# Queries and normalised x of items two to four transposed by DMA instead of TensorE, in a fused attention and maxout kernel

## The chip, the cores and the metric

The kernel runs on one core of a Trainium2 chip. The metric is device time in microseconds, the median of several executions. Lower is better. One execution is also taken by the profiler; all durations and waits below come from that one.

## What is computed

The input is a batch of 4 items with 8 heads, 768 tokens and 64 columns per head, and a sorting matrix of 8 by 8 per item and head. The reference, cut to what matters:

```python
for _ in range(5):                       # sort_net, 8x8 per head
    P = exp(P - max); P = P / rowsum; P = P / colsum
k_sorted = einsum('bhij,bhjcd->bhicd', P, k_b)   # blocks of 96 tokens mixed
v_sorted = einsum('bhij,bhjcd->bhicd', P, v_b)
scores = scale * matmul(q_b, k_sb^T)     # within a block of 96
attn = softmax(scores)
x = matmul(attn, v_sb)                   # -> 3072 tokens x 512
h1 = x @ w1; h2 = x @ w2
out = maximum(h1, h2) @ w_out            # float32, 3072 x 512
```

The kernel computes the last part as relu(x (w1 - w2)) @ w_out + x (w2 @ w_out). Products are in bfloat16 with float32 accumulation.

## The kernel before

The four items follow each other as a software pipeline. While TensorE does the dense products of item b (`moe_h`, the first layer, and `moe_out`, the second), it does the attention of item b+1 in between. The order is written out by hand: the loop at the end of the kernel has a list of `units` for item b (eight `moe_h`, then `moe_out` in halves of six products) with a cost each, and a list of `steps` for item b+1; after each unit so many steps are issued as the share of the units' cost that has passed asks for. `tail` holds steps that are tied to a certain unit, among them what is left of the item before. [...]PSUM is one pool of four tiles of two banks each, shared by all products, so a product waits when all four still wait for their eviction. `pick` shares the evictions out to ScalarE and VectorE by a running estimate of their load.

The steps of one item, with the lines before the change:

- `load_q` (L127), `load_k`, `load_v`: loads from DRAM on GpSimd's queue, which change float32 to bfloat16 on the way. There is one buffer for `q_raw` and one for `q_pair`, so the load of an item's queries waits for the pairing of the item before.
- `pair_q` (L322): VectorE copies the heads so that two heads that share a row group lie side by side: `q_pair` is 128 token groups by 4 head pairs by 6 rows by 128 columns. A partition holds six tokens that follow each other (R = 6).
- `sort_k`, `sort_v`, `sort_v_pair` (L365 to L428): the mixing of blocks on TensorE. `turn_v` (L203) turns the layout of v for it on VectorE or ScalarE.
- `q_transposes` (L332): 12 transposes on TensorE for each half of the heads into one PSUM tile, then one eviction into `qT`. In `qT` a block's 96 tokens lie as six groups of 16 (r, c).
- `scores` (L432): eight products of 96 columns into PSUM, then the exponential on ScalarE into an `e` tile. Its columns keep the (r, c) order.
- `values` (L458): eight products with the sorted v and a column of ones; then VectorE takes the reciprocal of the sum (L477) and multiplies (L483) into an `x` tile. An `x` tile serves two head pairs; the pool has three.
- `x_transposes` (L491): eight transposes on TensorE of 96 by 128, then an eviction into `xT` that also puts the tokens back in order (c, r).

Item one differs: its queries are transposed straight from `q_raw` at L349, and the kernel's beginning is written out without units.

`moe_h` of item b reads the first half of `xT` from its first unit on and the second half from unit five on. `moe_out` ends with an eviction into an `o` tile (three buffers) and a store of 512 KB on SP's queue (L613). Before the change SP's queue has one load and these stores alone.

In the steps of items two to four the values come as six groups inside the stage; the last two groups of values and the last two x transposes of an item stand in `tail`, in units 0, 1 and 2 of its own dense stage:

```python
tail = {0: [VA[6], VA[7]], 1: [TR[2]], 2: [TR[3]]}
```

Of the kernel before, what the change touches and what calls it, by code (L numbers as in the profile page):

```python
# [9 lines left out]

FP32 = mybir.dt.float32
BF16 = mybir.dt.bfloat16


@with_exitstack
def kernel(
# [16 lines left out]
    nc = tc.nc  # L33
# [4 lines left out]
    B, H, S, D = q.shape  # L38
    NB = sort_net.shape[-1]
    BLK = S // NB  # L40
# [5 lines left out]
    R = S // 128  # L46
    PB = 128 // NB
    HP = H // 2
    HB = BLK // 2
    TCH = S // 2  # L50
# [14 lines left out]
    def ps_f32(name):  # L65
        return psum.tile([128, 1024], FP32, tag="ps", name=name)

    def ps_bf16(name):
        return psum.tile([128, 2048], BF16, tag="ps", name=name)

# [5 lines left out]
    def keep_streaming(ps, n, by=None, width=512):  # L76

        w0 = fill[:, 0:128] if by is None else late[by]
        while n > 0:
            w = min(n, width)  # L80
            nc.tensor.matmul(ps[:, 0:w], w0, fill[:, 0:w], start=True, stop=True)  # L81
            n -= w
# [28 lines left out]
    q_raw, qT = {}, {}  # L111
# [10 lines left out]
    for n in range(NE):  # L122
        t = big.tile([BLK, 8 * BLK + 32], BF16, tag=f"e{n}", name=f"e{n}")
# [52 lines left out]
    ident = const.tile([128, 128], BF16, tag="ident", name="ident")  # L176
# [26 lines left out]
    def turn_v(rows, eng, c0, c1, d0=0, d1=D):  # L203
        dst = v_dc[rows, 0 : D * BLK].rearrange("p (d c) -> p d c", c=BLK)[:, d0:d1, c0:c1]
        src = v_raw[rows].rearrange("p (c d) -> p d c", d=D)[:, d0:d1, c0:c1]
        if eng == "A":
            nc.scalar.copy(out=dst, in_=src)
        else:
            nc.vector.tensor_copy(out=dst, in_=src)  # L209


    rowsum = const.tile([G, NB], FP32, tag="rowsum", name="rowsum")
# [107 lines left out]
    q_pair = {}  # L320
# [8 lines left out]
        )  # L329
        load["D"] += 900  # L330

    def q_transposes(b, half, eng=None, n=0):  # L332

        if half == 0:
            qT[b] = qpool.tile([128, HP, R, 128], BF16, tag="qT", name="qT")
        ps = ps_f32("tq_ps") if n else ps_bf16("tq_ps")
        keep_streaming(ps, n)
        if n:
            ps = ps.bitcast(BF16)
        for m in range(2 * R):  # L340
            hp, r = half * 2 + m // R, m % R
            c = slice(m * 128, (m + 1) * 128)
            if b in q_pair:
                nc.tensor.matmul(  # L344
                    ps[:, c], q_pair[b][:, hp, r], ident, is_transpose=True, start=True, stop=True
                )
                continue
            for h2 in range(2):
                nc.tensor.matmul(  # L349
                    ps[h2 * 64 : h2 * 64 + 64, c],  # L350
                    q_raw[b][:, hp + 4 * h2, r * D : (r + 1) * D],
                    ident,
                    is_transpose=True,
                    start=True,
                    stop=True,
                )
        evac(
            qT[b][:, half * 2 : half * 2 + 2].rearrange("p h r c -> p (h r c)"),
            ps[:, 0 : 2 * R * 128],
            2 * R * 128,  # L360
            two_x=True,
            eng=eng,
        )
# [68 lines left out]
    def scores(b, u, n=0):  # L432
        ih, hp = divmod(u, HP)
        ps = ps_f32("s_ps")
        keep_streaming(ps, n)
        for ii in range(4):
            i = ih * 4 + ii
            for h2 in range(2):
                rows = slice(h2 * 64, h2 * 64 + 64)
                rhs = qT[b][rows, hp, :, i * PB : (i + 1) * PB]  # L440
                nc.tensor.matmul(  # L441
                    ps[:, h2 * 512 + ii * BLK : h2 * 512 + (ii + 1) * BLK],
                    kT[b][rows, (hp * 8 + i) * BLK : (hp * 8 + i) * BLK + 128],
                    rhs,
                    start=True,
                    stop=True,
                )
        e = e_bufs[(b * 8 + u) % NE]
        nc.scalar.activation(  # L449
            out=e[:, 0 : 8 * BLK].rearrange("p (t f) -> p t f", t=2),  # L450
            in_=ps[0:BLK].rearrange("p (t f) -> p t f", t=2)[:, :, 0 : 4 * BLK],
            func=AF.Exp,
            scale=scale,
        )
        load["A"] += 800
        e_tiles[b, u] = e

    def values(b, u, n=0):  # L458
        ih, hp = divmod(u, HP)
        e = e_tiles.pop((b, u))  # L460
        m0 = (b % 2) * 64
        ps = ps_f32("o_ps")
        keep_streaming(ps, n)
        for h2 in range(2):
            for ii in range(4):
                nc.tensor.matmul(  # L466
                    ps[:, h2 * 512 + ii * 65 : h2 * 512 + (ii + 1) * 65],
                    e[:, (h2 * 4 + ii) * BLK : (h2 * 4 + ii) * BLK + 128],
                    v_sb[:, m0 + (hp + 4 * h2) * 8 + ih * 4 + ii, 0:65],
                    start=True,  # L470
                    stop=True,
                )
        ov = ps[0:BLK].rearrange("p (t f) -> p t f", t=2)[:, :, 0 : 4 * 65].rearrange(
            "p t (i f) -> p t i f", f=65
        )
        rs = xpool.tile([BLK, 2, 4], FP32, tag="rs", name="rs")
        nc.vector.reciprocal(out=rs, in_=ov[:, :, :, 64])  # L477
        if hp % 2 == 0:
            x_tiles[b, ih, hp // 2] = xpool.tile(
                [BLK, 2, 4, 2, D], BF16, tag="x", name="x", bufs=3  # L480
            )
        x = x_tiles[b, ih, hp // 2][:, :, :, hp % 2, :]
        nc.vector.tensor_tensor(  # L483
            out=x,
            in0=ov[:, :, :, 0:D],
            in1=rs.to_broadcast([BLK, 2, 4, D]),
            op=ALU.mult,
        )
        load["D"] += 900

    def x_transposes(b, t, eng=None):  # L491

        ih, hh = divmod(t, 2)
        ps = ps_bf16("tx_ps")
        x = x_tiles.pop((b, ih, hh))
        for m in range(8):
            h2, ii = divmod(m, 4)
            nc.tensor.matmul(  # L498
                ps[:, h2 * 1024 + ii * BLK : h2 * 1024 + (ii + 1) * BLK],
                x[:, h2, ii].rearrange("p n d -> p (n d)"),  # L500
                ident[0:BLK, 0:BLK],
                is_transpose=True,
                start=True,
                stop=True,
            )

        dst = xT[:, b % 2, ih, hh].rearrange("p h (i c r) -> p h i c r", r=R, c=PB)
        src = ps.rearrange("p (h f) -> p h f", h=2)[:, :, 0:TCH].rearrange(
            "p h (i r c) -> p h i c r", r=R, c=PB
        )  # L510
        evac(dst, src, 2 * TCH, eng=eng)


    w2T = big.tile([128, NFB, DMODEL], BF16, tag="w2T", name="w2T")
# [212 lines left out]
    for b in range(B):  # L727
# [25 lines left out]
        if b < B - 1:  # L753
            qs = [lambda half=half: q_transposes(b + 1, half) for half in range(2)]
            pairs = [lambda two=two: pair_q(b + 1, two) for two in range(2)]
            ks = [lambda t=t, b=b: sort_k(b + 1, t) for t in range(3)]
            SC, VA, TR = att(b + 1)

            def group(*fs):
                return [lambda: [f() for f in fs]]  # L760

            if b == 0:
                lo = 10
                tail[9][2:2] = ks
                vs = [lambda t=t: sort_v(1, t) for t in range(4)]
                tns = [lambda c=c: turn(both, c) for c in range(0, BLK, 12)]
                VA[1:6] = [(lambda f=f, g=g: (f(), g())) for f, g in zip(VA[1:6], tns)]
                TR[0:2] = [(lambda f=f, g=g: (f(), g())) for f, g in zip(TR[0:2], tns[5:])]
                SC[7:] = [lambda f=SC[7], g=tns[7]: (f(), g())]
                steps = group(*vs[:3]) + qs[:1] + group(*SC[0:2], vs[3]) + qs[1:] + VA[:1]  # L770
                steps += group(*SC[2:5]) + VA[1:2]
            elif b == 1:
                vs = [lambda t=t: sort_v_pair(2, t) for t in range(8)]
                steps = group(*pairs) + group(*ks) + qs[:1] + group(*SC[0:2], vs[0]) + qs[1:]
                steps += group(*vs[1:4]) + group(*vs[4:7]) + group(*SC[2:4], vs[7]) + VA[:2]
            else:
                steps = group(*pairs) + group(*ks) + qs + group(*SC[0:2])
                steps += VA[:1] + group(*SC[2:5]) + VA[1:2]
            rest = SC[4:] if b == 1 else SC[5:]
            steps += VA[2:3] + TR[:1] + VA[3:4]  # L780
            steps += group(*rest[:-1]) + TR[1:2] + VA[4:5] + rest[-1:] + VA[5:6]
        done = 0
        for n, unit in enumerate(units):
            unit()
# [4 lines left out]
            while done < min(want, len(steps)):  # L789
                steps[done]()  # L790
                done += 1
        tail = {0: [VA[6], VA[7]], 1: [TR[2]], 2: [TR[3]]}
        if b == 0:
            tail[3] = [lambda: load_k(3)]
            tail[8] = [lambda: load_q(3)]
# [28 lines left out]
```

The softmax here doesn't subtract the row's maximum and nothing guards it: scores larger than these inputs give would overflow.

## Time and profile before

| what | value |
|---|---|
| median of 3 runs | 178.54 us (178.17 to 178.55) |
| profiled execution | 178.51 us |
| its span in the trace | 176.5 us |
| instructions | 4808 |
| DMA queue 0 (loads, GpSimd) | 10304 packets, 12.58 MB, 42.4% of 16 engines |
| DMA queue 1 (SP) | 3328 packets, 6.10 MB, 9.1% of 16 engines |

The profiled execution's time is 2.0 us longer than its span: that part lies around the instructions of the trace. A row of instruction groups gives the line, the engine, the operation, output and input tiles with their shapes and the count; then the busy time in us and the mean ns of one; then the idle time of that engine just ahead of the group and what ended it. PE is TensorE's products, PEld its weight loads, DVE is VectorE, ACT is ScalarE, POOL is GpSimd, SP is SyncE, which has a queue of DMAs alone here. A timeline row begins with its start and its length in us. In the row of DMA digits each digit is a slice of a fortieth of the span, in tenths of full.

### The profile page before, as it was taken

Reading aid. Unit: us, or ns where it says so; the run is one execution under the profiler, and the core shown is the slowest. Engines: PE = TensorE matmul, PEld = TensorE weight load, DVE = VectorE, ACT = ScalarE, POOL = GpSimd, SP = SyncE. Lnnn points to the kernel's source line nnn. Section 1 sums busy time; section 2 is a strip of 40 time slices with the busy share of each in tenths; the row PEclk is TensorE's granted clock in tenths of the full one; section 3 lists DMA queues with packets and bytes.
Section 4 is the critical chain, followed back from the end, with each engine's and each line's share of the span. In section 5 each row is a group of like instructions: output and inputs, shape, how many; then the busy total and the mean of one; then the engine's idle time right before and its main releaser. Section 6 shows DMA issues by size and latency. Waiting matters only on the chain.

```text
span 176.5 us, 4808 instructions
## 1 busy us (share of the span) xinstructions
PE 169.4 (96%) x2159; PEld 105.1 (60%) x2159; DVE 95.3 (54%) x201; ACT 91.1 (52%) x110; POOL 24.1 (14%) x39
## 2 busy tenths in 40 slices
PE   7999999999999999999989999999999999999993
PEld 7848675655765554577655454677555546654453
DVE  4979758688555697354586435346325426240210
ACT  3689957854663655277783341474833232630021
POOL 7855353110730000020000000000000000000000
PEclk9999999999999999999999999999999999999999
DMA  4999999999799962039200203300001132000333
GB/s 55 200 205 208 198 207 215 201 203 210 114 214 212 206 176 108 16 119 148 38 0 4 97 26 119 119 6 4 0 0 62 61 119 111 12 0 0 119 116 125
DMA packets 13940, 19.19 MB, mean 109 GB/s; under 512 B 800, under 2 KB 8864, under 8 KB 13920
## 3 DMA queue, kind: packets, MB, share of 16 engines
q0 software_dynamic: 10304, 12.58, 42.4%
q1 hardware_dynamic: 3328, 6.10, 9.1%
q8 instruction: 17, 0.28, 0.6%
q10 hardware_dynamic: 288, 0.20, 0.3%
q14 instruction: 3, 0.02, 0.0%
HBM read 25.17 MB, written 6.29 MB: 178 GB/s over the span
## 4 chain that ended last, share of the span: by engine, by line
PE 84%; DVE 9%; ACT 4%; issue 1%; DMA 1%; ACTq 0%
PE out_ps L593 36%; PE h_ps L566 23%; PE o_ps L466 4%; PE k_ps L374 4%; PE wc_ps L544 4%; PE tx_ps L498 3%; PE s_ps L441 3%; PE tq_ps L344 2%; PE v_ps L395 2%; DVE g L582 1%; ACT w2T L103 1%; PE tw_ps L521 1%; DMA p_sb<-in_sort_net_dram 1%; PE tq_ps L349 1%; DVE x L483 1%
## 5 line engine op out<-in xcount | busy, mean ns | idle before, releaser
L593 PE MATMUL out_ps<-wo_sb,g 128*128 128x512 bf16 (+2 forms) x208 | 48.1, 363 | 0.3 <-DVE g L582 0.2
L566 PE MATMUL h_ps<-xT,w_sb 128*128 128x384 bf16 x256 | 45.8, 326 | 0.4 <-DVE g L582 0.2
L566 PEld LDWEIGHTS <-w_sb 128*128 128x128 bf16 x256 | 23.8, 98 | 15.1 <-issue 0.2
L449 ACT ACTIVATE e<-s_ps 96x768 bf16<-96x768 f32 x32 | 24.2, 803 | 12.2 <-PE s_ps L441 12.0
L580 ACT ACTIVATE g<-h_ps 128x768 bf16<-128x768 f32 x22 | 17.7, 811 | 21.8 <-PE h_ps L566 21.7
L593 PEld LDWEIGHTS <-g 128*128 128x128 bf16 x208 | 17.9, 97 | 15.9 <-issue 0.2
L593 PE MATMUL out_ps<-wc,xT 128*128 128x512 bf16 (+2 forms) x104 | 25.0, 362 | 0.0
L103 ACT COPY o<-out_ps 128x1024 f32<-128x1024 f32 x8 | 8.1, 1013 | 29.3 <-PE out_ps L593 25.6
L483 DVE TENSOR_TENSOR x<-o_ps,rs 96x512 bf16<-96x512 f32 x32 | 22.0, 687 | 1.1
L477 DVE RECIPROCAL rs<-o_ps 96x8 f32<-96x8 f32 x32 | 6.4, 201 | 25.5 <-PE o_ps L466 25.4
L582 DVE TENSOR_SCALAR g<-h_ps 128x768 bf16<-128x768 f32 x10 | 9.6, 957 | 15.7 <-PE h_ps L566 15.6
L593 PEld LDWEIGHTS <-xT 128*128 128x128 bf16 x104 | 9.9, 97 | 10.9
L209 DVE COPY v_dc<-v_raw 64x768 bf16<-64x768 bf16 (+2 forms) x18 | 15.6, 897 | 0.5 <-DMA v_raw<-in_v_dram 0.4
L466 PEld LDWEIGHTS <-e 96*128 96x128 bf16 x256 | 11.0, 98 | 5.6 <-ACT e L449 0.5
L466 PE MATMUL o_ps<-v_sb,e 96*128 96x65 bf16 x256 | 12.4, 193 | 0.3 <-DVE x L483 0.2
L103 ACT COPY xT<-tx_ps 128x768 bf16<-128x768 bf16 x13 | 10.4, 798 | 4.5 <-PE tx_ps L498 4.5
L105 DVE CAST v_sb<-v_ps 96x1024 bf16<-96x1024 f32 x7 | 8.5, 1215 | 5.3 <-PE v_ps L395 3.3
L103 ACT CAST v_sb<-v_ps 96x1024 bf16<-96x1024 f32 x9 | 8.7, 1014 | 2.3 <-PE v_ps L395 1.4
L103 ACT CAST kT<-k_ps 128x1024 bf16<-128x1024 f32 x10 | 9.6, 1026 | 0.5 <-PE k_ps L374 0.5
L441 PEld LDWEIGHTS <-kT 64*128 64x128 bf16 x256 | 6.1, 94 | 5.4 <-issue 4.6
L129 POOL DMA_DIRECT2D q_raw<-in_q_dram x4 | 3.6, 902 | 39.8 <-DVE q_pair L326 37.4
L81 PEld LDWEIGHTS <-fill 128*128 128x128 bf16 x109 | 7.7, 128 | 2.2 <-DVE fill L72 1.2
(77 smaller groups left out, 166.1 us busy)
## 6 DMA issues: line engine op xcount, KB each, us to landing
out_dram<-o SPq DMA_DIRECT2D x11, 512.0 KB, 2.8
k_raw<-in_k_dram POOLq DMA_DIRECT2D x12, 256.0 KB, 14.0
q_raw<-in_q_dram POOLq DMA_DIRECT2D x4, 768.0 KB, 9.7
v_raw<-in_v_dram POOLq DMA_DIRECT2D x6, 384.0 KB, 12.5
w_sb<-in_moe_w_dram POOLq DMA_DIRECT2D x3, 512.0 KB, 15.7
wo_sb<-in_moe_w_out_dram POOLq DMA_DIRECT2D x2, 512.0 KB, 19.4
v_raw<-in_v_dram POOLq DMA_DIRECT2D x3, 256.0 KB, 5.1
w_sb<-in_moe_w_dram POOLq DMA_DIRECT2D x2, 256.0 KB, 14.3
```

Source lines behind the costliest of these rows:

```text
L81: nc.tensor.matmul(ps[:, 0:w], w0, fill[:, 0:w], start=True, stop=True)
L103: nc.scalar.copy(out=out_ap, in_=in_ap)
L105: nc.vector.tensor_copy(out=out_ap, in_=in_ap)
L209: nc.vector.tensor_copy(out=dst, in_=src)
L441: nc.tensor.matmul(ps[:, h2 * 512 + ii * BLK : h2 * 512 + (ii + 1) * BLK], kT[b][rows, (hp * 8 + i) * BLK : (hp * 8 + i) * BLK + 128], rhs ...
L449: nc.scalar.activation(out=e[:, 0 : 8 * BLK].rearrange("p (t f) -> p t f", t=2), in_=ps[0:BLK].rearrange("p (t f) -> p t f", t=2)[:, :, 0 ...
L466: nc.tensor.matmul(ps[:, h2 * 512 + ii * 65 : h2 * 512 + (ii + 1) * 65], e[:, (h2 * 4 + ii) * BLK : (h2 * 4 + ii) * BLK + 128], v_sb[:, m0 ...
L483: nc.vector.tensor_tensor(out=x, in0=ov[:, :, :, 0:D], in1=rs.to_broadcast([BLK, 2, 4, D]), op=ALU.mult,)
L566: nc.tensor.matmul(h_ps[t][:, m * 512 : m * 512 + TCH], w1_sb[:, hp, fb * 128 : (fb + 1) * 128], xT[:, b % 2, ch, hp % 2, hp // 2, :], sta ...
L580: nc.scalar.activation(out=g, in_=src, func=AF.Relu)
L582: nc.vector.tensor_scalar(out=g, in0=src, scalar1=0.0, scalar2=None, op0=ALU.max)
L593: nc.tensor.matmul(dst, g_tiles[b, ch, m // 2][:, m % 2, off : off + 128] if m < NFB else xT[:, b % 2, ch, hp % 2, hp // 2, off : off + 12 ...
```

## The change

For items two to four the query transposes and the x transposes become DMA transposes on SP's queue, from SBUF to SBUF: one DMA per half of the heads for the queries (128 by 1536), one per `x` tile (96 by 1024). The products, their PSUM tiles and their evictions go. [...]the exponential now reads PSUM at a stride and writes `e` in token order, for all four items; x and `xT` then are in token order too, so item one's eviction of `xT` is a straight copy. Each of the eight score products gets its own 128 columns of PSUM instead of 96. The `x` pool has four tiles instead of three. The last two values groups and x transposes of items two to four move from `tail` into the item's own steps. `turn_v` gets a repeat count of 1, and `q_transposes` loses a parameter that no call uses.

```diff
     def turn_v(rows, eng, c0, c1, d0=0, d1=D):
...
+        for _ in range(TWICE):
+            if eng == "A":
+                nc.scalar.copy(out=dst, in_=src)
+            else:
+                nc.vector.tensor_copy(out=dst, in_=src)
...
-    def q_transposes(b, half, eng=None, n=0):
+    def q_transposes(b, half, eng=None):
 
         if half == 0:
             qT[b] = qpool.tile([128, HP, R, 128], BF16, tag="qT", name="qT")
-        ps = ps_f32("tq_ps") if n else ps_bf16("tq_ps")
-        keep_streaming(ps, n)
-        if n:
-            ps = ps.bitcast(BF16)
+        if b in q_pair:
+            nc.sync.dma_start_transpose(
+                out=qT[b][:, half * 2 : half * 2 + 2].rearrange("p h r c -> p (h r) c"),
+                in_=q_pair[b][:, half * 2 : half * 2 + 2].rearrange("p h r e -> p (h r e)"),
+            )
+            return
+        ps = ps_bf16("tq_ps")
         for m in range(2 * R):
...
-            if b in q_pair:
-                nc.tensor.matmul(
-                    ps[:, c], q_pair[b][:, hp, r], ident, is_transpose=True, start=True, stop=True
-                )
-                continue
...
-                    ps[:, h2 * 512 + ii * BLK : h2 * 512 + (ii + 1) * BLK],
+                    ps[:, h2 * 512 + ii * 128 : h2 * 512 + ii * 128 + BLK],
...
         nc.scalar.activation(
-            out=e[:, 0 : 8 * BLK].rearrange("p (t f) -> p t f", t=2),
-            in_=ps[0:BLK].rearrange("p (t f) -> p t f", t=2)[:, :, 0 : 4 * BLK],
+            out=e[:, 0 : 8 * BLK].rearrange("p (t c r) -> p t c r", t=8, r=R),
+            in_=ps[0:BLK].rearrange("p (t f) -> p t f", t=8)[:, :, 0:BLK].rearrange(
+                "p t (r c) -> p t c r", r=R
+            ),
...
-                [BLK, 2, 4, 2, D], BF16, tag="x", name="x", bufs=3
+                [BLK, 2, 4, 2, D], BF16, tag="x", name="x", bufs=4
...
         ih, hh = divmod(t, 2)
+        x = x_tiles.pop((b, ih, hh))
+        if b > 0:
+            nc.sync.dma_start_transpose(
+                out=xT[:, b % 2, ih, hh].rearrange("p h (i c) -> p (h i) c", c=BLK),
+                in_=x.rearrange("p h i n d -> p (h i n d)"),
+            )
+            return
         ps = ps_bf16("tx_ps")
...
-        dst = xT[:, b % 2, ih, hh].rearrange("p h (i c r) -> p h i c r", r=R, c=PB)
-        src = ps.rearrange("p (h f) -> p h f", h=2)[:, :, 0:TCH].rearrange(
-            "p h (i r c) -> p h i c r", r=R, c=PB
-        )
-        evac(dst, src, 2 * TCH, eng=eng)
+        src = ps.rearrange("p (h f) -> p h f", h=2)[:, :, 0:TCH]
+        evac(xT[:, b % 2, ih, hh], src, 2 * TCH, eng=eng)
...
+            steps[-1:] = group(steps[-1], TR[2]) + VA[6:7] + group(VA[7], TR[3])
...
-        tail = {0: [VA[6], VA[7]], 1: [TR[2]], 2: [TR[3]]}
+        tail = {}
```

More of the change, by code (lines that the diff above doesn't have):

```diff
@@ L12 @@
 BF16 = mybir.dt.bfloat16
+TWICE = 1
 @with_exitstack
@@ L205, in turn_v @@
         src = v_raw[rows].rearrange("p (c d) -> p d c", d=D)[:, d0:d1, c0:c1]
[L206 to L209, printed above, removed]
+        for _ in range(TWICE):
[3 more added lines that the diff above has]
+                nc.vector.tensor_copy(out=dst, in_=src)
     rowsum = const.tile([G, NB], FP32, tag="rowsum", name="rowsum")
@@ L493, in x_transposes @@
         ih, hh = divmod(t, 2)
+        x = x_tiles.pop((b, ih, hh))
[5 more added lines that the diff above has]
+            return
         ps = ps_bf16("tx_ps")
-        x = x_tiles.pop((b, ih, hh))
         for m in range(8):
```

## The prediction, made before the changed kernel was run

> **What bounds the kernel now.** I read the page's busy shares, then idle TensorE time by stage, then the order of work where items meet, then the groups the change touches, then DMA.
>
> ```profile
> PE 169.4 (96%) x2159; PEld 105.1 (60%) x2159; DVE 95.3 (54%) x201; ACT 91.1 (52%) x110; POOL 24.1 (14%) x39
> ...
> DMA  4999999999799962039200203300001132000333
> ```
>
> TensorE is busy 96% of the span, VectorE and ScalarE about half. The DMA digits (slices of 4.4 us) stay at 9 until about 57 us and rise to 9 again at 75 to 80. Busy share alone doesn't prove a bound; the stages do. Columns: length, PE, PEld, DVE, ACT, POOL busy, granted clock, DMA share, GB/s:
>
> ```profile
> 44.00:62.00 18.00, 17.65 (x306) 11.22 (x303) 10.63 (x16) 10.16 (x12) 4.62 (x8) 1.00 1.04 187
> ...
> 73.00:90.00 17.00, 16.61 (x297) 11.84 (x296) 8.71 (x12) 12.99 (x15) 0.90 (x1) 1.00 0.43 79
> ...
> 108.00:128.00 20.00, 19.65 (x287) 13.17 (x286) 8.99 (x15) 11.50 (x15) 0.00 (x0) 1.00 0.12 44
> ```
>
> In each, the stages in which items two to four are transposed, at most 0.4 us of TensorE is idle at full clock. So a product removed there is time removed, as long as nothing new makes TensorE wait. The timeline of the second such stage (start, length, engine, line, tiles):
>
> ```profile
> 76.36 0.51 PE L498 MATMUL tx_ps<-ident,x 96*128 96x96 bf16 x8
> 76.69 1.01 DVE L326 COPY q_pair<-q_raw 128x1536 bf16<-128x1536 bf16 x2
> 76.70 1.47 PE L566 MATMUL h_ps<-xT,w_sb 128*128 128x384 bf16 x8
> ...
> 78.00 0.90 POOL L129 DMA_DIRECT2D q_raw<-in_q_dram  x1 [28.05 <-DVE q_pair L326]
> ...
> 81.38 0.83 PE L344 MATMUL tq_ps<-ident,q_pair 128*128 128x128 bf16 x12
> ...
> 82.05 1.46 PE L566 MATMUL h_ps<-xT,w_sb 128*128 128x384 bf16 x8
> ...
> 83.53 0.52 PE L441 MATMUL s_ps<-qT,kT 64*128 64x96 bf16 x16
> ```
>
> Start to start, an x transpose group costs TensorE 76.70 - 76.36 = 0.34 us, half a query transpose 82.05 - 81.38 = 0.67. The scores that need the queries come only 2.1 us after. The next load of q goes out as soon as the pairing is done.
>
> ```profile
> L449 ACT ACTIVATE e<-s_ps 96x768 bf16<-96x768 f32 x32 | 24.2, 803 | 12.2 <-PE s_ps L441 12.0
> L580 ACT ACTIVATE g<-h_ps 128x768 bf16<-128x768 f32 x22 | 17.7, 811 | 21.8 <-PE h_ps L566 21.7
> L103 ACT COPY xT<-tx_ps 128x768 bf16<-128x768 bf16 x13 | 10.4, 798 | 4.5 <-PE tx_ps L498 4.5
> ...
> out_dram<-o SPq DMA_DIRECT2D x11, 512.0 KB, 2.8
> ...
> out_dram<-o SPq DMA_DIRECT2D x1, 64.0 KB, 1.7
> ```
>
> L103 reads PSUM in a permuted order, L580 straight: 798 and 811 ns for 768 columns, so the permuted read is free. A store lands 1.7 us (64 KB) to 2.8 us (512 KB) after its issue; I take 1.6 as fixed.
>
> [...]No DMA transpose is in this trace.
> - [...]In this stream TensorE needs 670/12 = 56 ns[...]
> - [...]
> - [...]the store at 61.0, beside loads, lands after 4.7 us instead of 2.8. It has 16 packets of 2 KB per DMA engine, and a load packet takes 116 ns (queue 0: 42.4% of 16 x 176.5 us over 10304): 16 x 0.116 = 1.9.
> - [...]
>
> **The change, part by part.**
>
> *Removed from TensorE.* Twelve x groups (items two to four, four each), at 0.34 to 0.44 us in the timeline: 4.2 us. Six query halves: 0.67, 0.70, 0.67, 0.67, and 1.34 for the last two: 4.05. Together 8.3 us, all on the path. Their evictions (twelve of about 0.8, six of 0.95 to 1.44) leave ScalarE and VectorE: nothing on the path, as both are half idle.
>
> *Exponentials.* 32 of 803 ns, now read at a stride: 0 by the L103 row. At 0.1 us more each, 3.2 us would lie on ScalarE, idle half the time; without that cover it would be 3.2. The contiguous xT copy of item one and the repeat count of 1: nothing.
>
> *Added on SP's queue: six query transposes (393 KB[...]) and twelve of x (197 KB[...]).* Landing time H of a query half: 1.6 fixed plus data. [...]I take 4.2, [...]a second half follows H - 1.6 later. [...]An x transpose: 2.9.
>
> *When the halves are due*, in the built instruction order:
> - Item two: pairing ends at 45.05 and SP has nothing ahead. Scores at 51.54 - 0.67 - 0.16 idle = 50.7. Landing 45.05 + 4.2 + 0.7 = 49.95. Second half 52.85; wanted at 54.2. No wait.
> - Item three: the pairing now stands right after the previous values, but SP's transposes stand behind the stage's last output store. Counted from the last output product: eviction 1.0 + issue 0.4, store issued; transposes at 1.8. The 2.7 us between that and the end of the store's data (4.7 - 1.6 - 0.4, beside the q load) hold back about 2.0 beyond their own start-up: landing 1.8 + 4.2 + 0.7 + 2.0 = 8.7. Scores at three h units 3.9 + sorting of keys 1.63 + two units 2.6 = 8.1. TensorE waits 0.6.
> - Item four: no load beside it, store data short: landing 1.8 + 0.1 + 4.2 = 6.1, due at 9.4; second half 8.7, due at 12.3. No wait.
>
> *x.* The last x group lands 0.9 (VectorE) + 2.9 after its values; due six units (7.8 us) or more later. SP waits for x with output stores behind it, but three output buffers cover about 1 us, and no engine waits for a store. Cost 0, and that of the fourth x buffer also 0; if cover were gone, 2.9 per group.
>
> *Moved.* The last two values groups of an item go from the next stage into its own: same products, no net cost. Steps come denser: six sort_v_pair fills now follow each other. They take 6 x 0.29 = 1.8 us, the evictions (1.01 on ScalarE, 1.22 on VectorE) three rounds of about 1.1; four PSUM tiles hold a part. I estimate 1.1 of waits against two of 0.24 now: +0.6 (bounds 0 and 1.5).
>
> *New lateness in item two.* VectorE's first second-pair turn (L209, 59.55) needs a v load issued at 47.3 that lands 11.5 us later, at 58.8. The two query halves take 0.79 MB from DMA engines that are full (about 0.21 MB/us written, twice that read): loads land 0.9 to 1.8 later. TensorE comes 1.4 earlier. VectorE waits, and behind that turn stand the x normalisations that free PSUM. I take 0.9 (bounds 0 and 2).
>
> *Sum.* Profiled execution 178.5 us (span 176.5 and 2.0 around it), 0.03 from the median 178.54, so no correction: 178.5 - 8.3 + 0.6 + 0.6 + 0.9 = 172.3. Low end: nothing given back, 170.2.
>
> **Rivals.**
> - *Half the gain is eaten (175.2).* H = 5.5: item two waits 0.55 for its first half and 1.0 for the second, item three 1.3 more: 172.3 + 2.85. [...]Against: nothing in the trace.
> - *The crossbar is slow (183.7, slower).* The place is the scores (L441) behind qT. At H = 7.4 [...]item two waits 2.45 and 2.9, item three 3.2 more than counted, item four 2.8 for its second half: 172.3 + 11.4. The waits reach 6.2 and cancel the gain at H of about 6.4; from there it is slower. [...]
> - *Blocks one after another (about 225).*[...]
> - *Nothing changes (178.5).* The removed products were covered anyway; the 0.4 us of idle time speaks against it.
>
> **Chances.** Forecast 172.3: 0.47, own range 170.2 to 174. Half eaten: 0.13. Slow crossbar: 0.29. Serial blocks: 0.08. Unchanged: 0.03. Within 0.2% is about what a measurement of this kernel can't tell from no change. Faster 0.60, same 0.03, slower 0.37. The range runs from 170.2 to 190, the slow case with H up to about 8; beyond lie the serial blocks and a little more.
>
> **What would show it.** Right: no tq_ps group, tx_ps in item one alone, TensorE idle under 1 us before any L441 group, query halves landing in 4 to 5 us. Wrong: waits for DMA ahead of the scores, a PE clock under 1, ScalarE's exponentials well over 803 ns, or, if landing is fast and little is gained, PSUM waits for VectorE around 60 us.

## The result, and the profile after it

The changed kernel takes 194.67 us (median of 4 runs, 194.04 to 196.8) against 178.49 for the kernel before in the same comparison. The ratio is 1.093, 95% interval 1.085 to 1.102: slower, and beyond the end of the predicted range (190). The profiled execution took 194.95 us, its span 192.9 us, 16.4 longer than before. Where one of a kernel's runs was over 1.5% slower than its fastest, its median below leaves that run out. Lines of the changed kernel are five or so further on than before: the products of `h_ps` are L571, those of `out_ps` L598; the scores are still L441.

From the page of the changed kernel: busy shares, granted clock, DMA share by slice (of 4.8 us here), SP's DMA queue, and two groups.

```profile
PE 163.8 (85%) x1972; PEld 97.7 (51%) x1991; DVE 87.2 (45%) x192; ACT 83.4 (43%) x101; POOL 23.0 (12%) x39
...
PEclk9999999999978556999996999999999999999998
DMA  4999999999999940536995002555900336300223
...
q1 hardware_dynamic: 22336, 10.82, 23.8%
...
L449 ACT ACTIVATE e<-s_ps 96x768 bf16<-96x768 f32 x32 | 24.2, 803 | 35.4 <-PE s_ps L441 35.2
...
L441 PE MATMUL s_ps<-qT,kT 64*128 64x96 bf16 x256 | 9.1, 211 | 18.2 <-DMA qT<-q_pair 17.9
```

TensorE is busy 85% instead of 96%. TensorE's idle time grew from 7.1 to 29.1 us, and one group has most of the growth: 18.2 us ahead of the scores, 17.9 of it ended by the DMA that transposes the queries. The exponentials take 803 ns as before, so reading PSUM at this stride cost nothing here. The clock, 9 throughout before, drops to 7, 8, 5, 5, 6 between 53 and 77 us, and to 6 at 101 us. And SP's queue has 22336 packets where it had 3328.

The chain of waits says the same (the share of the span by what held it up):

```profile
PE 66%; DMA 18%; DVE 10%; ACT 2%; issue 2%; SPq 0%; ACTq 0%
PE out_ps L598 32%; PE h_ps L571 19%; DMA qT<-q_pair 18%; PE o_ps L468 4%; PE k_ps L374 3%; PE s_ps L441 2%; PE wc_ps L549 1%; PE v_ps L395 1%; DVE g L587 1%; ACT w2T L104 1%; PE tw_ps L526 1%; PE tq_ps L349 1%; DMA p_sb<-in_sort_net_dram 1%; DVE x L485 1%; DVE colsum L228 1%
```

TensorE's timeline shows where the 17.9 us lie. The bracket is the idle time ahead of the row and what ended it.

```profile
53.40 0.51 PE L441 MATMUL s_ps<-qT,kT 64*128 64x96 bf16 x16 [2.84 <-DMA qT<-q_pair]
...
70.59 1.14 PE L441 MATMUL s_ps<-qT,kT 64*128 64x96 bf16 x24 [11.22 <-DMA qT<-q_pair]
...
102.59 0.55 PE L441 MATMUL s_ps<-qT,kT 64*128 64x96 bf16 x16 [3.81 <-DMA qT<-q_pair]
```

Items two (two halves of the heads) and three (first half) wait; item four doesn't. SP's timeline gives the other end, two transposes to a row, and the query transposes' own view their durations on SP (shortest, median, longest) and their landing:

```profile
45.38 12.57 SPq L339 DMA_TRANSPOSE qT<-q_pair  x2
...
92.09 9.61 SPq L339 DMA_TRANSPOSE qT<-q_pair  x2
...
133.06 4.26 SPq L339 DMA_TRANSPOSE qT<-q_pair  x2
```

```profile
L339 SPq DMA_TRANSPOSE qT<-q_pair x6: 1510/2903/11006, 45.4 to 135.5; - x6
...
  PE s_ps L441: 17.9, 3
...
DMA to landing us min/median/max: 4.1/6.7/23.6
```

Half by half, from issue to landing: item two 8.0 and 23.6 us, item three 10.4 and 5.4, item four 4.8 and 4.1. Six like DMAs, up to nearly six times apart. The windows show what else ran (columns as in the windows of before: length, busy time of the five engines, clock, DMA share, GB/s):

```profile
50.00:58.00 8.00, 4.61 (x50) 2.50 (x50) 2.91 (x4) 1.50 (x2) 0.26 (x1) 0.82 1.23 169
58.00:71.00 13.00, 1.78 (x17) 0.78 (x17) 0.42 (x1) 0.00 (x0) 0.00 (x0) 0.63 0.97 160
71.00:79.00 8.00, 7.57 (x71) 4.06 (x66) 4.44 (x9) 3.22 (x4) 0.00 (x0) 0.71 0.01 2
...
97.00:106.00 9.00, 5.19 (x51) 2.92 (x50) 1.22 (x1) 4.06 (x6) 0.00 (x0) 0.83 0.84 158
```

Where a half is late the DMA engines are full, with loads. From 58 to 71 us TensorE does 1.8 us of work and ScalarE none, yet the DMA share is 0.97. When the wait is over (71 to 79) DMA is idle and TensorE full, at a clock of 0.71: the wait is paid a second time, in slow products.

**The sum of the 16.4 us.** Removed products -8.3 (the prediction's count). Waits for `qT` +17.9. Slow clock: in the records of the trace the granted clock is either full or half while products run, and half in three stretches, each behind a wait (columns as above):

```profile
55.16:58.58 3.42, 3.20 (x16) 1.46 (x16) 1.37 (x3) 0.20 (x1) 0.00 (x0) 0.50 0.98 170
61.99:75.64 13.65, 4.73 (x46) 2.90 (x48) 1.62 (x3) 2.20 (x3) 0.00 (x0) 0.50 0.61 90
...
102.95:106.36 3.41, 3.41 (x34) 1.81 (x28) 1.22 (x1) 1.58 (x3) 0.00 (x0) 0.50 0.09 18
```

Products take about twice as long in them. Six like products in the second stretch, and behind it:

```profile
72.46 2.75 PE L598 MATMUL out_ps<-wo_sb,g 128*128 128x512 bf16 x6
...
76.84 1.46 PE L598 MATMUL out_ps<-wo_sb,g 128*128 128x512 bf16 x6
```

So half of TensorE's busy time there is lost: (3.2 + 4.73 + 3.41) / 2 = 5.7 us, an estimate. Together +15.3, which leaves about 1.1 for everything else. The 1.6 us lost in the first stretch only shorten the wait that follows it, as that wait ends when the second half lands. By themselves the slow products thus lengthen the kernel by some 4.1 us (2.4 + 1.7).

**Why the transfers are late.** SP's queue has 22336 - 3328 = 19008 more packets. Six query halves of 128 x 12 rows and twelve x tiles of 96 x 8 rows, each row of 128 columns (256 bytes), are 9216 + 9216 = 18432, and 18 DMAs by 32 packets of 4 bytes that report the end are 576: the sum fits to the packet. So in the records a DMA transpose goes row by row: 1536 packets for a query half, 96 per DMA engine if they are spread evenly over the 16. Packets started per us on the 16 engines, counted from the DMA records of the trace of the changed kernel (the loads' 4-byte end reports, some 11 per us at 57 to 61, are among the load packets):

```
us   load packets, mean ns   transpose rows (256 bytes)
48            0                    810     alone
50          236,  85                 0     load of q
51          243,  81                 0     load of q
57           40, 345                41     loads of v and k
59           48, 367                48     loads of v and k
61           47, 313                48     loads of v and k
94          173, 114                 0     load of q
137           0                    875     alone
```

Alone, a half's 1536 rows pass in about 2 us (875 in the us from 137 on, 21 ns each). Beside the loads of v and k (packets of 2 KB, 0.19 us, and of 6 KB, 0.54 us on the mean between 53.5 and 70 us) as many rows start as load packets. That fits turns of one for one, 41 rows to 40 load packets at 57 us: each row would then cost about a whole load packet of waiting, and that 96 times, an estimate from these counts. (The records don't name the DMA engine, so the order of the turns isn't seen.) Beside the load of q (1024 packets of 768 bytes) SP's queue gets almost nothing: no row in the slices at 50, 51 and 94 us, against 236, 243 and 173 load packets. The first half of item two shows it at its purest: its 1536 rows have all started by 49.84, but of its 32 end reports the first goes at 51.0 and the last at 53.0, it lands at 53.4, and the first row of the second half starts at 52.27. With that load held back (the run with the loads of item two held, below) the same reports go at 48.8 to 49.1 and the second half's rows follow at once. In item three an output store that SP issued at 91.62 has its first packet at 96.2, 4.6 us later where other stores take 0.9, and the transposes behind it follow at 98.7.

So taking turns fits the counts beside v and k, and not those beside q. What keeps SP's queue off beside q was not shown: no run varied the packets of that load.

### The profile page after: what moved, and what is told of

Read it like the earlier page. It is cut to its first block, busy times and chain, and to the rows that moved or that the text cites. A ratio compares the mean times of both kernels' runs of the same rounds, so it can differ in the third digit from the quotient of the medians.

```text
span 192.9 us, 4483 instructions
## 1 busy us (share of the span) xinstructions
PE 163.8 (85%) x1972; PEld 97.7 (51%) x1991; DVE 87.2 (45%) x192; ACT 83.4 (43%) x101; POOL 23.0 (12%) x39
## 3 DMA queue, kind: packets, MB, share of 16 engines
q1 hardware_dynamic: 22336, 10.82, 23.8%
## 4 chain that ended last, share of the span: by engine, by line
PE 66%; DMA 18%; DVE 10%; ACT 2%; issue 2%; SPq 0%; ACTq 0%
PE out_ps L598 32%; PE h_ps L571 19%; DMA qT<-q_pair 18%; PE o_ps L468 4%; PE k_ps L374 3%; PE s_ps L441 2%; PE wc_ps L549 1%; PE v_ps L395 1%; DVE g L587 1%; ACT w2T L104 1%; PE tw_ps L526 1%; PE tq_ps L349 1%; DMA p_sb<-in_sort_net_dram 1%; DVE x L485 1%; DVE colsum L228 1%
## 5 line engine op out<-in xcount | busy, mean ns | idle before, releaser
L598 PE MATMUL out_ps<-wo_sb,g 128*128 128x512 bf16 (+2 forms) x196 | 49.0, 376 | 1.9 <-issue 0.4
L571 PE MATMUL h_ps<-xT,w_sb 128*128 128x384 bf16 x256 | 45.5, 333 | 0.0
L571 PEld LDWEIGHTS <-w_sb 128*128 128x128 bf16 x256 | 24.6, 99 | 17.0 <-issue 1.5
L598 PEld LDWEIGHTS <-g 128*128 128x128 bf16 x208 | 18.4, 100 | 17.6 <-issue 2.5
L585 ACT ACTIVATE g<-h_ps 128x768 bf16<-128x768 f32 x24 | 19.4, 812 | 17.1 <-PE h_ps L571 17.1
L598 PE MATMUL out_ps<-wc,xT 128*128 128x512 bf16 (+2 forms) x103 | 25.0, 365 | 0.1
L441 PE MATMUL s_ps<-qT,kT 64*128 64x96 bf16 x256 | 9.1, 211 | 18.2 <-DMA qT<-q_pair 17.9
L104 ACT COPY o<-out_ps 128x1024 f32<-128x1024 f32 x7 | 7.1, 1012 | 39.6 <-PE out_ps L598 34.3
L587 DVE TENSOR_SCALAR g<-h_ps 128x768 bf16<-128x768 f32 x8 | 7.7, 958 | 23.6 <-PE h_ps L571 23.6
L441 PEld LDWEIGHTS <-kT 64*128 64x128 bf16 x256 | 6.4, 98 | 23.3 <-DMA qT<-q_pair 15.0
L468 PEld LDWEIGHTS <-e 96*128 96x128 bf16 x256 | 12.1, 101 | 7.3 <-issue 1.4
L598 PEld LDWEIGHTS <-xT 128*128 128x128 bf16 x104 | 10.0, 99 | 11.5 <-issue 1.0
L468 PE MATMUL o_ps<-v_sb,e 96*128 96x65 bf16 x256 | 13.8, 199 | 0.7 <-DVE x L485 0.3
L104 ACT CAST kT<-k_ps 128x1024 bf16<-128x1024 f32 x11 | 10.4, 1024 | 0.5 <-PE k_ps L374 0.5
L106 DVE COPY o<-out_ps 128x1024 f32<-128x1024 f32 x4 | 4.9, 1224 | 8.8 <-PE out_ps L598 8.8
## 6 DMA issues: line engine op xcount, KB each, us to landing
k_raw<-in_k_dram POOLq DMA_DIRECT2D x12, 256.0 KB, 15.3
```

The source lines that it names most:

```text
L104: nc.scalar.copy(out=out_ap, in_=in_ap)
L106: nc.vector.tensor_copy(out=out_ap, in_=in_ap)
L441: nc.tensor.matmul(ps[:, h2 * 512 + ii * 128 : h2 * 512 + ii * 128 + BLK], kT[b][rows, (hp * 8 + i) * BLK : (hp * 8 + i) * BLK + 128], rhs ...
L468: nc.tensor.matmul(ps[:, h2 * 512 + ii * 65 : h2 * 512 + (ii + 1) * 65], e[:, (h2 * 4 + ii) * BLK : (h2 * 4 + ii) * BLK + 128], v_sb[:, m0 ...
L571: nc.tensor.matmul(h_ps[t][:, m * 512 : m * 512 + TCH], w1_sb[:, hp, fb * 128 : (fb + 1) * 128], xT[:, b % 2, ch, hp % 2, hp // 2, :], sta ...
L585: nc.scalar.activation(out=g, in_=src, func=AF.Relu)
```

## The experiments

Medians; the kernel before took 178.28 to 178.36 us beside them. All kernels start from the changed one.

**Each half of the change alone.** Queries back on TensorE (the removed branch of `q_transposes` restored), x by DMA:

```diff
-        if b in q_pair:
+        if b >= 4:
             nc.sync.dma_start_transpose(
```

> Queries of all items on TensorE, x of items two to four by DMA. Theory packets: x transposes have 48 packets per DMA engine and are due 8 us later, so they cost nothing and 4.2 us of products go: none_dma minus 4.2, about 174.5 to 175.3. Rival crossbar (any DMA transpose on SP's queue slows the kernel): 178.5 or more, with waits for xT.

Measured: 176.53 us, ratio 0.990 (0.988 to 0.991). No wait for `xT`, landing near 3 us, clock 1.00: the x transposes by DMA do no harm, and the whole loss is the queries'. But the gain is 1.8 us where 3 or more was expected. Two windows whose counterparts of before are shown above:

```profile
44.00:62.00 18.00, 17.03 (x291) 10.68 (x284) 11.00 (x16) 10.04 (x12) 4.62 (x8) 1.00 1.07 190
...
73.00:90.00 17.00, 15.89 (x302) 10.77 (x300) 5.28 (x7) 12.25 (x15) 0.90 (x1) 1.00 0.56 95
```

Idle time of TensorE is 0.97 and 1.11 us, where it was 0.35 and 0.39: part of the removed products came back as idle time in pieces of under 0.7 us, ended by ScalarE (exponentials, the eviction of `qT`) and VectorE.

**Everything on TensorE again, the rest of the change kept** (as above, and in the x steps):

```diff
-        if b > 0:
+        if b > 3:
             nc.sync.dma_start_transpose(
```

> Leaves both kinds of transposes on TensorE and keeps the rest of the change (exponentials in token order, score products 128 columns apart, four x tiles, the last values and x groups in the item's own steps). Theory packets (the loss is query DMAs whose 256-byte packets take turns with load packets): nothing of the loss is here, 178.5 to 179.5. Rival order (the denser steps and the strided exponential carry a good part of the loss): 181 or more, with exponentials over 803 ns or waits for PSUM.

Measured: 191.83 us, ratio 1.076 (1.070 to 1.081), far above the expected range and on the side of the rival about the order. TensorE's largest wait (in all, count, longest):

```profile
PE tx_ps L511 <- DVE x L490: 8.6, 6, 2.0
```

The moved steps put an x transpose right behind the values whose `x` VectorE has yet to normalise. TensorE, in order, waits up to 2.0 us each time, 8.6 in all, of 12.3 that the span grew. A stretch of 3.4 us at half clock (151.5 to 154.9) adds up to 1.7; the rest wasn't taken apart. "Moved: no net cost" thus holds only while the transposes aren't TensorE's: there SP does the waiting (up to 15.2 us ahead of an x transpose in the changed kernel), with nothing urgent behind it.

**Which loads?** Item two's queries on TensorE, items three and four by DMA (`if b >= 2:`):

> As changed, but item two's queries back on TensorE; items three and four and all x by DMA. Theory packets: the waits of item two (2.8 and 11.2 us) go with the slow clock behind them (about 3), 1.4 of products comes back: 194.7 - 14.1 - 3 + 1.4 = 179. Item three still waits 3.8 and its half lands in 10 us. Rival crossbar: item three, now the first query transposes in the queue, shows the long landing instead (20 us and more for its second half), 188 or more.

Measured: 179.43 us, ratio 1.005 (1.002 to 1.008). The halves land after 4.7 to 10.3 us, and of two waits for them one is long (in all, count, longest):

```profile
PE s_ps L446 <- DMA qT<-q_pair: 4.1, 2, 3.8
```

Then the same with the next load of q held back until item three's second half has landed. A tiny GpSimd sum reads a column of `q_raw` and one of the transposed queries, and the load stands behind it on GpSimd's queue:

```diff
+    def gate(b):
+        nc.gpsimd.tensor_tensor(out=gate_sb[:, b : b + 1],
+            in0=q_raw[b][:, 0, 0:1], in1=qT[b][:, 3, 0, 0:1], op=ALU.add)
...
-            tail[8] = [lambda: load_q(3)]
+            tail[8] = [lambda: gate(2), lambda: load_q(3)]
```

> As q34, and the next load of q (768 KB), which ran beside item three's query transposes, is held by a small GpSimd operation that reads the transposed queries. Theory packets: item three's first half lands in 5 to 6.5 us (the store ahead stays) instead of 10.4, no wait or under 0.5 us before its scores: q34 minus 3.8 and minus about 1.2 of slow clock, 174. Rival store (item three is late because the 512 KB store stands ahead in the queue): landing stays at 9 to 10 us and the time at q34's.

Measured: 173.82 us, ratio 0.975 (0.972 to 0.977). Only the time of one load has changed (and the sum of 0.19 us ahead of it), and the wait is gone:

```profile
L339 SPq DMA_TRANSPOSE qT<-q_pair x4: 1430/1894/2774, 76.0 to 116.1; - x4
...
DMA to landing us min/median/max: 4.5/4.8/5.8
```

TensorE isn't among the waiters for `qT`; only the gate is. A transfer of the same size, shape and queue lands in 4.5 us instead of 10.3, behind the same store. The bytes, the way of transposing and the store ahead are not the cause, the load beside them is.

**The other way round: a load added.** Item four's halves landed in 4.8 and 4.1 us with nothing beside them. Here one more load of q (its data unused) goes out beside them:

```diff
-                steps = group(*pairs) + group(*ks) + qs + group(*SC[0:2])
+                steps = group(*pairs, lambda: load_q(3)) + group(*ks) + qs + group(*SC[0:2])
```

> The changed kernel, with one more load of the same 768 KB of q, issued after item four's pairing, into the buffer that nobody reads any more. Only item four, whose halves landed in 4.8 and 4.1 us with no load beside them, is touched. Theory packets (rows of 256 bytes get few turns beside a load): its first half lands in about 10 us as item three's did; due after 7.9, so TensorE waits 2 to 3 and works slowly for about 1 more: 198 to 199. Rival (items two and three were late because of the store, the crossbar or their place in the program): no change, 194.7.

Measured: 196.0 us, ratio 1.102 (1.096 to 1.107). Item four's halves now land after 9.8 and 5.4 us, and its scores wait for the first time (TensorE's timeline):

```profile
140.38 0.52 PE L441 MATMUL s_ps<-qT,kT 64*128 64x96 bf16 x16 [1.98 <-DMA qT<-q_pair]
```

The landing is as expected and the wait at the low end. The total stays under the expected 198 to 199: it is 1.3 us over the changed kernel, within the spread of the two (195.6 to 197.7 and 194.0 to 196.8), so the trace shows the effect, the total doesn't.

**All queries by DMA, the loads of item two held back.** The gate stands before the loads of q and v in item two and q in item three:

```diff
+                held = [lambda: gate(1), lambda: load_q(2), lambda: load_v(2), lambda: load_v(3)]
+                steps += group(*qs[1:], *held) + VA[:1]
```

> All queries by DMA as changed, but the loads of q and v that ran beside item two's transposes, and the load of q beside item three's, are each held until both halves have landed. Theory packets: item two's halves land in about 5 us each instead of 8.0 and 23.6, no wait over 1 us for queries; but the v loads come 6 to 7 us later, and VectorE, which turns v, waits with the x work behind it: 172.5 plus 2 to 6, 175 to 178. Rival crossbar (the second half of a pair is slow by itself): waits of 10 us for queries stay, over 185.

Measured: 182.69 us, ratio 1.024 (1.021 to 1.027). All six halves land in 4.1 to 5.6 us. But the v loads come late instead (TensorE's waits, VectorE's timeline and the landing of the queries, three views):

```profile
PE o_ps L480 <- DVE x L497: 7.3, 2, 7.1
```

```profile
66.73 0.81 DVE L211 COPY v_dc<-v_raw 128x768 bf16<-128x768 bf16 x1 [8.74 <-DMA v_raw<-in_v_dram]
```

```profile
L339 SPq DMA_TRANSPOSE qT<-q_pair x6: 1527/1896/2557, 45.4 to 123.9; - x6
...
DMA to landing us min/median/max: 4.1/4.9/5.6
```

VectorE waits in order for v ahead of its turning, the normalisation of `x` stands behind that, and TensorE's next values wait for that. The clock is at half from 65.1 to 75.3 us, with 5.7 us of products in it, up to 2.8 us more. An x transpose issued at 61.4, beside the held loads, lands only after 13.1 us, where those of the changed kernel take 2.8 to 4.3. In the two orders tried, either the queries or the v loads of item two are late. The expected 175 to 178 had priced the late v too low and left the clock out.

**The clock by itself.** To tell slow products from the waits, products with zeros were put ahead of the three groups of scores that wait, 11, 49 and 16 of 512 columns, so that TensorE stays busy while it waits:

```diff
+    FILL = {(1, 0): 11 * 512, (1, 2): 49 * 512, (2, 0): 16 * 512}
...
-        SC = [lambda u=u: scores(b, u) for u in range(8)]
+        SC = [lambda u=u: scores(b, u, FILL.get((b, u), 0)) for u in range(8)]
```

> The changed kernel, with products of zeros (the result is thrown away) put ahead of the three score groups that waited for queries: 11, 49 and 16 products of 512 columns, 2.4, 10.6 and 3.5 us at full clock, each shorter than the wait it stands in. Theory clock (besides the 17.9 us of waits, the waits lower TensorE's clock and the work behind them runs slow for about 5 us): the clock stays at 1 and 194.7 falls to 189 to 191, with landings unchanged. Rival (the lower clock is only recorded during the idle time and costs nothing): 194 to 196.

Measured: 195.98 us, ratio 1.097 (1.090 to 1.104), in the rival's range, but it settles nothing. The second half landed after 25.6 us instead of 23.6, the wait outlasted the products by 4.75 us and the clock fell all the same. So 66 instead of 49:

> As fill, with 66 products of zeros instead of 49 ahead of the second wait: in fill that wait outlasted them by 4.8 us and the clock fell again. Theory clock: with the 14.3 us covered, the clock stays at 1 in the items' stages and the time falls by the slow work behind the waits, counted from the stages as about 5 us, less what the products themselves run over (0 to 1 us): 189.5 to 191.5. Rival (the clock costs little, and the cost lies in the landings alone): 194 or more.

Measured: 192.18 us, ratio 1.080 (1.075 to 1.084), with

```profile
PEclk9999999999999999999999999999999999999999
```

That lies between the two ranges. With the clock up, the kernel takes 194.67 - 192.18 = 2.5 us less, though the second half landed 1.2 us later still (24.8). The slow clock cost 2.5 to 3.7 us, then, about what the 4.1 estimated above says. The size is rough, as the intervals of the two ratios (1.085 to 1.102 and 1.075 to 1.084) barely part. Most of the loss is waiting.

**Where the last part of the expected gain went.** In the version with the held q load, 178.35 - 4.2 (x) - 2.7 (queries of items three and four) would be 171.5; it takes 173.8. Two tries. First, the old `tail` and its order restored:

> As q34_late, with the last two values and x groups of items two to four back in units 0 to 2 of the item's own dense stage. Theory dense (the denser steps cost about 1 us of PSUM waits in item two's stage and x transposes have cover to spare: they land in 3 us and are due 4 us later): 172.5 to 173.3. Rival cover (the move was needed: xT or the queries, which now stand behind these x transposes on SP's queue, come too late): 174.5 or more, with waits for DMA ahead of L571 or the scores.

Measured: 173.46 us, ratio 0.973 (0.972 to 0.974); TensorE waits 1.2 us for `qT` and 0.4 for `xT` that it didn't wait for otherwise, and these may hide a gain. Then, with the new order, the sorting of v and the scores spread more evenly:

```diff
-                steps += group(*SC[2:5]) + VA[1:2]
+                steps += group(*SC[2:4]) + VA[1:2]
...
-                steps = group(*pairs) + group(*ks) + qs[:1] + group(*SC[0:2], vs[0]) + qs[1:]
-                steps += group(*vs[1:4]) + group(*vs[4:7]) + group(*SC[2:4], vs[7]) + VA[:2]
+                steps = group(*pairs) + group(*ks, *qs) + group(*vs[:3]) + group(*SC[0:2], vs[3])
+                steps += group(*vs[4:6]) + group(*vs[6:]) + group(*SC[2:4]) + VA[:2]
...
-            rest = SC[4:] if b == 1 else SC[5:]
+            rest = SC[4:] if b < 2 else SC[5:]
```

> As q34_late, with the steps of items two and three regrouped: item two's third to fifth scores no longer stand in one step ahead of a values group, and the empty places that the query transposes leave among item three's steps are filled with sort_v_pair groups, so that six no longer follow each other. No product is added or removed. Theory dense (about 1.3 us of PSUM waits come from the denser order: 0.6 and 0.3 in item two's stage, 0.3 and 0.2 in item three's): 172.5 to 173.3, below q34_late's 173.8. Rival (the rest of the missing gain lies elsewhere): 173.6 to 174.

Measured: 173.71 us, ratio 0.974 (0.972 to 0.976). Neither moves the time by more than its spread. Spreading the steps in this way gains nothing, so the density of the sorting isn't shown to be the cause; the moved groups aren't either, though the new waits leave that less certain. The trace of the version with the held q load tells a part of the place: from item one's first `moe_h` product to item two's it takes 50.5 us, the kernel before 49.5, with 0.8 us more idle time of TensorE. What takes these 2.3 us, of which 1.5 were in the prediction, stays open. These three kernels are about 2.6% faster than before, and the best that came out.

## Why the prediction was wrong, step by step

- *Removed 8.3 us*: it fits, but no run measures it alone. With the waits (17.9) and the slow clock (5.7, an estimate) taken out of the changed kernel, 192.9 - 23.6 + 2.0 = 171.3 is left; the forecast had 172.3.
- *Exponentials at a stride 0*: right, 803 ns.
- *Landing of a query half, H = 4.2*: right where nothing runs beside: 4.1 and 4.8 in item four, and 4.1 to 5.6 with the loads held. So the rivals "crossbar" (a transpose that is slow by itself, H = 7.4) and "blocks one after another" are both refuted. The 4.2 was the author's estimate, and nothing in the trace of before showed it; that it fits is luck. What took the time here is rows: 96 x 22 ns = 2.1 us (21 to 23 ns each in the slices at 137 and 48 us).
- *The 0.7 for a load beside, in the landings of items two and three*: **this is the step that failed.** It is 6 packets per DMA engine at 0.116 us; the 0.116 was measured, the 6 was the author's estimate. The unit was wrong: the records have 96 row packets per DMA engine. The alternation fits beside v and k (41 rows to 40 load packets), but not beside q (none to 236). The prediction's own 0.116 us then gives 96 x 0.116 = 11.1 us, and the v and k packets of that moment are longer than that mean. The measured lateness is 23.6 - 4.2 = 19.4 us for the second half. For the first, and in item three, taking turns doesn't explain it: beside the load of q SP's queue moved next to nothing for 2.4 us (49.84 to 52.27) and 3.7 us (4.6 less the usual 0.9).
- *Item two no wait, item three 0.6, item four none*: 2.84 + 11.22, 3.81, and none. All of the first two follow from the failed step, the price of a load beside; the last was right, and for the stated reason (no load beside it). Two small slips in the working change nothing here: the DMA digits are read a slice early (the 9s last until 61.8 us, but for a 7, and come back at 79.4 to 83.8), and item two's second half, 4.2 - 1.6 after the first, would land at 52.55, not 52.85.
- *x transposes 2.9, no wait*: right in this kernel, 2.8 to 4.3, and TensorE doesn't wait for them. It holds for their places, not for x transposes as such: beside the held v loads one took 13.1.
- *Moved groups no net cost*: right in this kernel, but not a property of the move: with TensorE transposing, there are 8.6 us of waits in the same order.
- *Denser sorting 0.6, lateness of v 0.9*: 1.5 together against about 1.1 left over in the sum, and 2.3 in the version with the held q load, which has no long waits. The causes named are not confirmed; spreading the sorting gained nothing.
- *Slow clock*: the prediction has no price for it, only "a PE clock under 1" as a sign. The clock halved after the waits of 2.84 and 3.81 us, within that of 11.22, and in the run with an added load after 1.98 us. In that same run a wait of 2.93 us, of which 1.77 fall into the stretch in the first row below, left it at full (columns as above):

```profile
99.82:103.23 3.41, 1.64 (x38) 1.26 (x39) 0.78 (x1) 1.19 (x2) 0.00 (x0) 1.00 0.88 190
103.23:106.64 3.41, 3.17 (x87) 2.10 (x86) 1.99 (x3) 2.33 (x4) 0.00 (x0) 1.00 0.00 0
...
137.37:140.78 3.41, 1.43 (x23) 0.79 (x20) 0.96 (x1) 0.64 (x1) 0.00 (x0) 1.00 1.16 209
140.78:144.19 3.41, 3.41 (x24) 1.84 (x19) 0.58 (x1) 1.50 (x2) 0.00 (x0) 0.50 0.09 18
```

The half-clock stretches between the products of the changed kernel last 3.41, 13.65 and 3.41 us. With its span cut at their edges into stretches of 3.41 us, these three drops from full to half follow stretches with 1.98, 2.62 and 3.05 us of idle TensorE in all, and a fourth, at 191.70 us, one with 2.03; the other stretches at full clock have 1.34 us or less. In the rows above a drop follows 1.98 us and none follows 1.77. So the idle time within such a stretch fits these drops; the length of a single gap doesn't. The slow clock cost 2.5 to 3.7 us in the changed kernel.

The slower rival had the right place, L441 behind `qT`, and the right chain of effects. Its cause, a transfer that is slow by itself, was wrong, and so was its size: it couldn't tell item two from item four.

## What to carry to other kernels

A DMA's time alone said little about it beside loads: 4.1 us alone, up to 23.6 beside them. Count its packets per DMA engine (96 rows for a query half, if spread evenly), and price each at a packet of whatever load will run beside it (0.19 to 0.54 us for v and k); beside the load of q, where SP's queue stood for 2.4 and 3.7 us, even that was too low. A transpose by DMA was many small packets here; put it where no large load is in flight, or hold the load until it has landed (10.3 us became 4.5 with the load of q held), and then check what needed that load (the v loads held cost a wait of 7.1 us). When a step leaves an in-order engine for a queue, moving it closer to its producer may be free, as in the changed kernel, where TensorE didn't wait for `xT`; the same order may be dear if the step ever goes back (8.6 us of waits).

## What the runs showed that was not expected

- A DMA transpose SBUF to SBUF went in rows of 256 bytes, about 22 ns a packet alone. Beside load packets of 0.19 to 0.54 us as many rows as load packets started.
- A load with 768-byte packets held SP's queue off for 2.4 and 3.7 us, even the end reports of a transfer whose rows had all started.
- A DMA transpose occupies SP itself: a query half 1.4 to 2.9 us with no load beside it, but 11.0 for the second half of item two, in which SP issues nothing else.
- A wait of 1.98 us was followed by 3.41 us at half clock, while one of 2.93 us, split over two stretches of 3.41 us, wasn't.
